# A transformer block on one core: key tiles by contraction halves, more transposes by DMA, and a new order

## The chip, the core and the metric

The kernel runs on one of the eight cores of a Trainium2 chip. The metric is device time in microseconds (us), the median of three runs, as reported for the core. TensorE (PE) multiplies, VectorE (DVE) and ScalarE (ACT) do elementwise work and move results out of PSUM, GpSimd (POOL) makes masks, and SyncE (SP) issues all DMAs. Each engine runs its own list of instructions strictly in order and waits for the others by semaphores.

## The reference, cut to what matters

The input x has 2048 tokens of width 512; the two weight chains are a linear attention with 32 heads of 16 and a dense layer of width 1792 with relu. All tensors are bf16.

```python
qkv = layernorm(x) @ wqkv
phi = lambda t: where(t > 0, t + 1, exp(t)) + 1e-6
pq, pk = phi(q), phi(k)
kv = einsum("bhsd,bhse->bhde", pk, v);  z = einsum("bhsd->bhd", pk)
o  = einsum("bhqd,bhde->bhqe", pq, kv) / (einsum("bhqd,bhd->bhq", pq, z) + 1e-6)
h  = x + merge_heads(o) @ wo
out = h + relu(layernorm(h) @ w1) @ w2
```

## The kernel before, in words

Tokens lie in 16 tiles of 128 and in four chunks (c) of 512. Every step is a small function `op_<name>`; the string ORDER (line 18) lists them as words, name and arguments joined by dots, and the loop in lines 548 to 550 calls them one after the other. A word goes to the engine that its operation uses, and each engine executes its own words in the order in which they stand. A scheduler doesn't come into it (line 92 sets a manual schedule). So ORDER is the whole plan: for each engine a queue, and between the queues the data dependences. PSUM has eight banks; the bank is an argument of the word, and a matmul that writes a bank waits until the last reader of its former contents is through.

The words of this text, with engine and line of the operation:

- lx.t.n loads n tiles of x (SP, L201); lk, lq, lv, lo, l1, l2 load weights (SP, L204).
- S.t, A.t: statistics of the first norm (DVE, L226, L227). R.t.n: its 1/sqrt, two ACT operations (L232, L233). N.t: the normalised tile ln_nat (DVE, L251).
- T.t.b transposes a normalised tile on PE, four 128x128 transposes into bank b (L270), and E.t (ACT, L280) or V.t (DVE, L283) copies it out into lnT. X.t does the same without PE: one transposing DMA (SP, L291).
- K.t.b: keys of a tile, four matmuls of 512 columns, one for each 128 of the contraction (L299). K.t.b.k.n does n of the four, beginning with k, so that a tile's keys can be cut into halves; the halves add up in the same bank.
- F, U, M, D: phi of the keys, exp and relu on ACT (L317, L320), min and add on DVE (L324, L327). qF, qU, qM, qD are the same for the queries; qW (DVE, L332) takes relu and add in one operation from PSUM and needs no qU.
- G.t: 512x512 sum over the tokens of normalised x times pk, four matmuls, in banks 4 to 7 (L351). The values are not computed for each token: kv (L392) multiplies G by the value weights afterwards, after gA (ACT) or gD (DVE, L387) moved G out. za, zf, z, zc, zh make the sums of the keys.
- Q.c.j.b: a quarter of the queries of a chunk, transposed, four matmuls (L307).
- dn.c.b: denominators of a chunk, 16 matmuls of 8 columns (L448); dnl, dnx (ACT, L454, L461) make the reciprocals, spread over the head's 16 columns, in rn (which lies in wk_sb); dt.t transposes a tile of them by DMA into rd (SP, L480). rt.t.b does that on PE (L270), and re.t (ACT, L472) copies it out. dm.c.jb.n (DVE, L484) multiplies two quarters of the queries by rd.
- m, mA, mD: kv times the output weights (L404). h.t.b: attention output of a tile, four matmuls (L494); hD (DVE, L500) adds x.
- s.t, a.t, r, n.t: second norm (DVE L228, L229, ACT L232, DVE L258). x.t transposes by DMA (SP, L292); t.t.b and e.t do it by PE and ACT (L286).
- p.c.f.b: first dense layer, four matmuls (L510); pA (ACT, L516) and pD (DVE, L521) apply the relu to two. f.t.b.f0.n: second dense layer (L530), in two halves of seven matmuls; fo (DVE, L538) scales and adds, fd (SP, L545) stores.
- warm.n.b: n matmuls of zeros ahead of the work (L215).

Of the kernel before, what the change touches and what calls it, by code (L numbers as in the profile page):

```python
# [15 lines left out]


ORDER = """
const table lx.0.1 lx.2.1 S.0 lx.1.1 S.2 A.0 S.1 A.2 R.0.1 N.0 R.2.1 lx.3.1 lk.0.2 lx.4.2 masks warm.1.7
warm.9.7 A.1 R.1.1 T.0.6 S.3 warm.1.7 N.2 T.2.4 N.1 A.3 E.0 R.3.1 T.1.5 lk.2.2 S.4 E.1 N.3 A.4 V.2 S.5 A.5  # L20
K.0.6 lx.6.2 K.1.3 T.3.1 F.0.1 U.0.1 lx.8.4 E.3 K.2.0 M.0.1 S.6 D.0.1 K.3.2 A.6 S.7 F.1.1 M.1.1 lx.12.4 R.4.2
N.5 A.7 N.4 U.1.1 D.1.1 F.2.1 U.2.1 R.6.2 S.8 S.9 N.7 A.9 A.8 M.2.1 N.6 lq.0.2 G.0 T.5.1 E.5 T.4.3 G.1 X.7
K.5.1 D.2.1 E.4 K.4.0 R.8.2 T.6.3 G.2 N.9 X.9 F.3.1 U.3.1 S.12 N.8 S.13 X.8 lq.2.2 M.3.1 A.13 A.12 D.3.1 E.6
K.6.2 F.4.2 R.12.2 U.4.2 K.7.3 G.3 M.4.2 S.11 F.6.2 U.6.2 N.12 D.4.2 S.10 S.14 N.13 M.6.2 A.11 A.10 D.6.2 A.14
R.10.2 X.12 K.9.1 G.4 N.11 S.15 N.10 A.15 X.13 K.8.0 G.5 G.6 za.2 U.8.2 F.8.2 X.11 X.10 G.7 R.14.2 K.13.1
K.12.0 M.8.2 N.15 D.8.2 za.4 N.14 K.11.3 K.10.2 G.8 l2.0.3 F.12.2 U.12.2 za.6 X.15 X.14 Q.0.0.0 F.10.2 Q.0.1.1
lv.2.2 l1.0.2 M.12.2 lv.0.2 l2.10.4 U.10.2 qU.0.0.2 qF.0.0.2 M.10.2 za.8 D.12.2 D.10.2 za.10 za.12 K.14.2 G.9
K.15.3 F.14.2 U.14.2 G.10 Q.0.3.1 Q.0.2.0 M.14.2 qF.0.2.2 qU.0.2.2 G.11 zf.12 D.14.2 G.12 z.0.2.14 z.2.2.14
z.1.2.14 z.3.2.14 qM.0.2.2 l2.7.3 lo.0.2 lo.2.2 l1.2.2 qM.0.0.2 qD.0.2.2 G.13 zc G.14 qD.0.0.2 zh dn.0.0 G.15
gD.2.2 gD.0.2 Q.1.1.3 Q.1.0.2 dnl.0 dnx.0.0.2 Q.1.2.0 dnx.0.2.2 kv.3.4 kv.0.4 kv.1.4 kv.2.4 Q.1.3.1 qF.1.0.2  # L30
qM.1.0.2 kx qF.1.2.2 qW.1.0.2 dt.0 dt.3 dt.2 dt.1 m.2.6 m.1.5 m.3.7 m.0.4 mA.0.2 Q.2.0.2 Q.2.1.3 qM.1.2.2
mA.2.2 qW.1.2.2 dn.1.5 dm.0.0.2 dm.0.2.2 dnl.1 dnx.1.2.2 Q.2.3.1 h.3.5 hD.3 h.0.6 h.1.7 hD.0 s.3 dnx.1.0.2
dt.6 Q.2.2.0 dt.4 dt.7 dt.5 qF.2.0.2 qU.2.0.2 h.2.6 hD.1 Q.3.0.2 Q.3.1.3 s.0 qF.2.2.2 qU.2.2.2 s.1 qU.3.0.2
a.3 a.0 hD.2 qM.2.0.2 n.0 a.1 n.1 dm.1.0.2 dm.1.2.2 n.3 s.2 Q.3.2.0 Q.3.3.1 qD.2.0.2 a.2 qM.2.2.2 n.2 qF.3.0.2
qF.3.2.2 l2.3.4 x.0 qM.3.2.2 qD.2.2.2 h.5.6 h.7.7 h.6.5 x.1 t.2.3 r.0.4 e.2 h.4.4 x.3 dn.2.3 dnl.2 dnx.2.0.2
p.0.0.2 dt.8 hD.6 qM.3.0.2 qW.3.2.2 hD.4 p.0.1.3 qD.3.0.2 hD.5 dnx.2.2.2 pA.0.0.2 p.0.3.1 p.0.2.0 dn.3.6
pD.0.2.2 p.0.5.3 p.0.4.2 pD.0.4.2 p.0.7.1 p.0.6.0 p.0.13.3 s.6 dt.10 p.0.12.2 dt.11 dt.9 hD.7 a.6 s.5 dm.2.0.2
dm.2.2.2 dnl.3 pA.0.6.2 a.5 pD.0.12.2 f.2.6.0.7 s.7 h.11.7 h.9.0 p.0.9.3 h.8.5 p.0.8.2 dnx.3.2.2 dnx.3.0.2
hD.9 a.7 hD.11 p.0.10.0 f.3.7.0.7 p.0.11.1 h.10.4 dt.15 pA.0.10.2 pD.0.8.2 dt.14 dt.13 dt.12 s.4 s.9 n.5
dm.3.2.2 s.11 hD.8 a.11 dm.3.0.2 hD.10 n.7 f.2.6.7.7 h.13.5 h.15.4 n.6 hD.15 a.4 n.4 s.8 h.14.1 f.3.7.7.7  # L40
h.12.2 f.0.4.0.7 x.5 x.6 s.10 hD.14 a.10 hD.13 hD.12 n.10 x.4 s.13 s.12 x.7 n.11 a.9 a.8 f.1.5.0.7 a.12 s.15
p.1.1.1 p.1.0.0 pA.1.0.2 f.1.5.7.7 a.15 s.14 fo.2 p.1.8.0 p.1.9.1 n.12 a.13 fo.3 n.15 n.13 fo.1 pD.1.8.2
f.0.4.7.7 a.14 n.8 p.1.12.0 p.1.13.1 p.1.2.2 p.1.3.3 p.1.10.6 r.12.4 r.4.4 pA.1.12.2 n.9 x.11 x.15 x.10 x.9
x.8 pD.1.2.2 p.1.7.5 p.1.5.1 fd.2 fd.3 p.1.4.0 p.2.3.3 p.2.2.2 n.14 fo.0 pD.1.4.2 pD.2.2.2 fd.0 x.13 x.14
p.2.0.0 p.1.11.7 p.2.7.3 p.2.1.1 r.8.4 pA.2.0.2 p.2.6.2 p.1.6.4 pD.2.6.2 p.2.4.0 pA.1.10.2 pA.1.6.2 p.2.5.1
pA.2.4.2 f.7.7.0.7 p.2.12.0 p.2.13.1 f.4.4.0.7 f.5.5.0.7 p.2.10.2 f.4.4.7.7 p.2.11.3 f.6.6.0.7 pD.2.10.2
pD.2.12.2 fd.1 x.12 f.6.6.7.7 f.5.5.7.7 p.2.8.0 p.2.9.1 p.3.2.2 p.3.3.3 fo.6 pD.2.8.2 fo.4 fo.5 p.3.4.0
f.7.7.7.7 p.3.5.1 pA.3.4.2 pD.3.2.2 fo.7 f.10.6.0.7 p.3.1.1 f.9.5.0.7 p.3.7.3 p.3.0.0 f.8.4.0.7 p.3.6.2 fd.6
f.9.5.7.7 f.11.7.0.7 f.10.6.7.7 fd.4 fd.5 fd.7 pA.3.0.2 pA.3.6.2 f.8.4.7.7 p.3.12.0 fo.9 f.11.7.7.7 p.3.13.1
p.3.11.3 p.3.10.2 pD.3.10.2 fo.8 fo.11 pA.3.12.2 p.3.9.1 f.13.5.0.7 p.3.8.0 f.12.4.0.7 pA.3.8.2 fo.10 fd.10  # L50
fd.9 f.13.5.7.7 f.14.6.0.7 fo.13 f.12.4.7.7 f.15.5.0.14.3.1 f.14.6.7.7 f.15.7.0.14.0.2 fd.13 fd.8 fd.11 fo.12
fo.14 fo.15.3.1 f.15.4.0.14.2.1 fd.12 fd.14 fd.15.3.1 fo.15.0.2 fo.15.2.1 fd.15.0.2 fd.15.2.1
"""


# [525 lines left out]
```

## Time and profile before

| What | Value |
|---|---|
| three runs | 170.04, 170.34, 170.82 us |
| median | 170.34 us |
| span of the profiled execution, first to last instruction | 168.6 us |
| what lies around the span, median less span | 1.74 us |
| DVE, ACT, POOL busy | 104.7, 64.3, 4.8 us |
| DMA moved | 15.36 MB |

All times in the trace are counted from the start of the span. A row of the chain of waits reads: start, length, what was running or being waited for. A row of the timeline reads: start, length, engine, line, operation, tiles, count, and in brackets the idle time of the engine before it and who ended it. A row of a group reads: line, engine, operation, tiles, shapes, count, then busy time, mean ns of one, then idle time before. A row of DMA issues ends with the median time from issue to landing. PE is TensorE's matmul row, PEld its weight loads, SPq the queue of SyncE.

### The profile page before, as it was taken

How to read it: one execution, taken by the hardware profiler on the slowest of the kernel's cores; microseconds unless marked ns; L12 is line 12 of the kernel's file. 1: busy time of each engine (PE TensorE's matmuls, PEld its weight loads, DVE VectorE, ACT ScalarE, POOL GpSimd, SP SyncE). 2: the span in 40 equal slices, each digit the busy share in tenths (PEclk: the TensorE clock that was granted, in tenths of full speed). 3: DMA queues.
4: the chain of work that ended last, by engine and by line, in shares of the span. 5: the costliest groups of instructions: out<-in, count | busy, mean ns of one | idle time of the engine just before them, and what ended most of it. 6: DMA issues, size and time to landing. Idle time of an engine off the chain costs nothing.

```text
span 168.6 us, 2307 instructions
## 1 busy us (share of the span) xinstructions
PE 163.1 (97%) x875; PEld 76.3 (45%) x875; DVE 104.7 (62%) x207; ACT 64.3 (38%) x97; POOL 4.8 (3%) x21
## 2 busy tenths in 40 slices
...
DMA packets 30091, 15.36 MB, mean 91 GB/s; under 512 B 22656, under 2 KB 29056, under 8 KB 30080
## 3 DMA queue, kind: packets, MB, share of 16 engines
...
q8 instruction: 7, 0.11, 0.3%
...
HBM read 7.86 MB, written 2.10 MB: 59 GB/s over the span
## 4 chain that ended last, share of the span: by engine, by line
PE 84%; ACT 4%; DMA 4%; SPq 3%; DVE 2%; issue 1%; DVEq 0%; ACTq 0%
PE bk L530 29%; PE bk L510 29%; PE bk L351 7%; PE bk L299 7%; PE bk L494 6%; PE bk L307 5%; DMA wk_sb<-in_A_wqkv_dram 3%; ACT eb L317 1%; DMA rd<-wk_sb 1%; SPq L201 1%; SPq L480 1%; PE bk L448 1%; ACT rb L320 1%; DVE pqT L332 1%; ACT lnT L280 1%
## 5 line engine op out<-in xcount | busy, mean ns | idle before, releaser
L530 PE MATMUL bk<-w_sb,at 128*128 128x512 bf16 (+2 forms) x252 | 51.5, 355 | 0.0
L510 PE MATMUL bk<-lnT,w_sb 128*128 128x512 bf16 x224 | 51.4, 379 | 0.0
L516 ACT ACTIVATE at<-bk 128x1024 bf16<-128x1024 f32 x14 | 14.1, 1023 | 70.3 <-PE bk L510 70.3
L521 DVE TENSOR_SCALAR at<-bk 128x1024 bf16<-128x1024 f32 x14 | 17.0, 1221 | 33.7 <-PE bk L510 33.7
L530 PEld LDWEIGHTS <-at 128*128 128x128 bf16 x252 | 23.6, 98 | 25.2
L510 PEld LDWEIGHTS <-w_sb 128*128 128x128 bf16 x224 | 21.8, 98 | 26.0 <-issue 0.2
L538 DVE SCALAR_TENSOR_TENSOR gT<-bk,rstd,h_nat 128x512 bf16<-128x512 f32 (+2 forms) x18 | 12.0, 686 | 18.3 <-PE bk L530 15.9
L317 ACT ACTIVATE eb<-bk 128x1024 bf16<-128x1024 f32 (+1 forms) x18 | 16.5, 925 | 6.1 <-PE bk L299 3.5
L299 PE MATMUL bk<-wk_sb,lnT 128*128 128x512 bf16 x64 | 15.5, 379 | 0.6 <-DMA wk_sb<-in_A_wqkv_dram 0.5
L494 PE MATMUL bk<-m_sb,pqs 128*128 128x512 bf16 x64 | 15.5, 379 | 0.1
L307 PE MATMUL bk<-lnT,wq_sb 128*128 128x512 bf16 x64 | 15.1, 379 | 0.1
L320 ACT ACTIVATE rb<-bk 128x1024 bf16<-128x1024 f32 (+1 forms) x15 | 13.6, 906 | 1.2 <-PE bk L307 1.2
L351 PE MATMUL bk<-at,h_nat 128*128 128x512 bf16 x56 | 13.7, 379 | 0.0
L500 DVE TENSOR_TENSOR h_nat<-bk,x_nat 128x512 bf16<-128x512 f32 x16 | 10.8, 678 | 2.7 <-PE bk L494 2.6
L226 DVE BATCH_NORM_STATS2 st<-x_nat 128x6 f32<-128x512 bf16 x16 | 10.6, 678 | 1.8 <-DMA x_nat<-in_A_x_dram 1.8
L228 DVE BATCH_NORM_STATS2 st<-h_nat 128x6 f32<-128x512 bf16 x16 | 10.5, 679 | 0.0
L299 PEld LDWEIGHTS <-lnT 128*128 128x128 bf16 x64 | 5.9, 98 | 8.2 <-ACT lnT L280 1.2
L494 PEld LDWEIGHTS <-pqs 128*128 128x128 bf16 x64 | 6.1, 98 | 7.9 <-DVE pqs L484 1.2
L307 PEld LDWEIGHTS <-wq_sb 128*128 128x128 bf16 x64 | 6.1, 97 | 7.3 <-issue 0.4
L351 PEld LDWEIGHTS <-h_nat 128*128 128x128 bf16 x64 | 6.0, 98 | 6.6
L461 ACT ACTIVATE wk_sb<-ld 128x1024 bf16<-128x1024 f32 x8 | 8.0, 1048 | 0.1
L324 DVE TENSOR_SCALAR eb<-eb 128x1024 bf16<-128x1024 bf16 (+1 forms) x18 | 6.9, 388 | 1.2 <-ACT eb L317 1.1
...
## 6 DMA issues: line engine op xcount, KB each, us to landing
...
wk_sb<-in_A_wqkv_dram SPq DMA_DIRECT2D x2, 256.0 KB, 3.7
x_nat<-in_A_x_dram SPq DMA_DIRECT2D x2, 256.0 KB, 4.1
```

The lines of the kernel that those rows point to most:

```text
L299: nc.tensor.matmul(bk[:, b, :], lhsT=lnT[c][:, kd, j * P : (j + 1) * P], rhs=wk_sb[:, kd, :], start=(kd == 0), stop=(kd == KD - 1),)
L307: nc.tensor.matmul(bk[:, b, :], lhsT=wq_sb[:, kd, j * P : (j + 1) * P], rhs=lnT[c][:, kd, :], start=(kd == 0), stop=(kd == KD - 1),)
L317: nc.scalar.activation(out=buf(eb, kind, i, n), in_=bank(at_bank[kind, i], n), func=ACT.Exp)
L320: nc.scalar.activation(out=buf(rb, kind, i, n), in_=bank(at_bank[kind, i], n), func=ACT.Relu)
L351: nc.tensor.matmul(bk[:, KD + kd, :], lhsT=ln_nat[:, t, kd * P : (kd + 1) * P], rhs=pk(t)[:, 0, :], start=(t == 0), stop=(t == NT - 1),)
L494: nc.tensor.matmul(bk[:, b, :], lhsT=pqs[:, (c * KD + jb) % NQ, j * P : (j + 1) * P], rhs=m_sb[:, jb, :], start=(jb == 0), stop=(jb == KD ...
L500: nc.vector.tensor_tensor(out=h_nat[:, t : t + n, :], in0=bank(at_bank["h", t], n), in1=x_nat[:, t : t + n, :], op=ALU.add,)
L510: nc.tensor.matmul(bk[:, b, cols], lhsT=w1_sb[:, kd, f * P : (f + 1) * P], rhs=lnT[c][:, kd, cols], start=(kd == 0), stop=(kd == KD - 1),)
L516: nc.scalar.activation(out=acts[c % 2][:, f : f + n, :], in_=bank(at_bank["p", c, f], n), func=ACT.Relu)
L521: nc.vector.tensor_scalar(out=acts[c % 2][:, f : f + n, :], in0=bank(at_bank["p", c, f], n), scalar1=0.0, scalar2=None, op0=ALU.max,)
L530: nc.tensor.matmul(bk[:, b, 0 : w * P], lhsT=acts[c % 2][:, f, j * P : (j + 1) * P], rhs=w2_sb[:, f, k * P : (k + w) * P], start=(f == 0), ...
L538: nc.vector.scalar_tensor_tensor(out=o_t[:, t % NO, cols], in0=bk[:, at_bank["f", t, k], 0 : w * P], scalar=rstd2[:, t : t + 1], in1=h_nat ...
```

## The change

Only ORDER is changed, in every line. Its parts:

- T.4, T.5, T.6 with their copies E.4, E.5, E.6 become X.4, X.5, X.6. Tile 2 is transposed first, and its copy is E.2 (ACT) in place of V.2 (DVE).
- K.0, K.1 and K.2 are cut into halves of two matmuls: first the first halves of tiles 2, 0, 1, then T.3, then the second halves, then K.3.
- t.2 with its copy e.2 becomes x.2. dt.1 and dt.2 become rt.1, re.1 and rt.2, re.2.
- One of two gD becomes gA, one of two mA becomes mD; qD.0.2 with qU becomes qW, and two qW become qU with qD; some pA and pD change places.
- The order of nearly all words is another, on PE, DVE, ACT and SP; the banks are assigned anew. lx.4.2 goes ahead of lk.0.2; lq.0.2 and lq.2.2 go behind X.12; the loads of wo, wv, w1 and w2 are put elsewhere between the transposes.

The words of the first part, before and after, cut to what the prediction speaks of:

```diff
-const table lx.0.1 lx.2.1 S.0 lx.1.1 S.2 A.0 S.1 A.2 R.0.1 N.0 R.2.1 lx.3.1 lk.0.2 lx.4.2 masks warm.1.7
-warm.9.7 A.1 R.1.1 T.0.6 S.3 warm.1.7 N.2 T.2.4 N.1 A.3 E.0 R.3.1 T.1.5 lk.2.2 S.4 E.1 N.3 A.4 V.2 S.5 A.5
-K.0.6 lx.6.2 K.1.3 T.3.1 F.0.1 U.0.1 lx.8.4 E.3 K.2.0 M.0.1 S.6 D.0.1 K.3.2 A.6 S.7 F.1.1 M.1.1 lx.12.4 R.4.2
-N.5 A.7 N.4 U.1.1 D.1.1 F.2.1 U.2.1 R.6.2 S.8 S.9 N.7 A.9 A.8 M.2.1 N.6 lq.0.2 G.0 T.5.1 E.5 T.4.3 G.1 X.7
-K.5.1 D.2.1 E.4 K.4.0 R.8.2 T.6.3 G.2 N.9 X.9 F.3.1 U.3.1 S.12 N.8 S.13 X.8 lq.2.2 M.3.1 A.13 A.12 D.3.1 E.6
...
+lx.2.1 table lx.0.1 const S.2 S.0 A.2 A.0 masks lx.1.1 R.2.1 lx.3.1 lx.4.2 S.1 lk.0.2 N.2 warm.9.5 A.1 R.0.1
+lk.2.2 lx.6.2 N.0 R.1.1 S.3 N.1 A.3 S.5 T.2.0 E.2 warm.1.5 T.0.3 S.4 A.5 T.1.2 E.0 K.2.0.0.2 lx.8.4 A.4 R.3.1
+E.1 N.3 lx.12.4 R.4.2 K.0.7.0.2 K.1.2.0.2 T.3.1 K.0.7.2.2 E.3 U.0.1 N.5 N.4 F.0.1 S.7 S.6 M.0.1 X.5 A.6 A.7 X.4
+K.2.0.2.2 K.1.2.2.2 U.1.1 D.0.1 R.6.2 S.9 N.6 S.8 K.3.3 warm.1.5 X.6 F.2.1 N.7 M.2.1 U.2.1 U.3.1 A.8 F.3.1 F.1.1
+D.2.1 A.9 G.0 M.3.1 S.12 X.7 R.8.2 K.5.1 N.9 K.4.0 D.3.1 G.2 X.9 K.6.2 F.4.2 G.3 K.7.3 N.8 S.13 A.12 M.1.1 U.4.2
+A.13 D.1.1 R.12.2 U.6.2 F.6.2 X.8 G.1 K.9.1 M.4.2 N.13 N.12 K.8.0 D.4.2 S.11 S.10 A.11 S.15 M.6.2 A.10 G.4 G.5
+X.13 X.12 F.8.2 R.10.2 U.8.2 D.6.2 M.8.2 lq.0.2 A.15 S.14 N.11 N.10 lq.2.2 G.7 A.14 X.11 X.10 za.2 lo.0.2 D.8.2
+K.13.2 R.14.2 K.12.1 G.6 G.8 K.11.3 za.4 U.12.2 F.12.2 N.14 N.15 M.12.2 za.6 lv.2.2 X.15 X.14 za.8 D.12.2 l1.2.2
...
```

The order of each engine is read from this by taking its words alone. SP's new order up to the first dt, and PE's from the queries of chunk 1 to the first p, are:

```
SP: lx.2 lx.0 lx.1 lx.3 lx.4 lk.0 lk.2 lx.6 lx.8 lx.12 X.5 X.4 X.6 X.7 X.9 X.8 X.13 X.12 lq.0 lq.2 X.11 X.10 lo.0 lv.2 X.15 X.14 l1.2 l1.0 lv.0 lo.2 dt.3 dt.0 l2.10 dt.4 dt.7 dt.6 dt.5 x.2 x.1 x.3 x.0
PE: z (4) G.14 G.15 dn.0 Q.1 (4) kv (4) rt.2 rt.1 Q.2.1 m (4) dn.1 Q.2.0 Q.2.3 h.2 h.1 h.3 Q.2.2 Q.3.3 h.0 Q.3.2 Q.3.1 Q.3.0 h.7 h.6 h.5 h.4 dn.2 p.0.1
```

PE's order before in the same stretch, from dn.0, was: dn.0 G.15 Q.1.1 Q.1.0 Q.1.2 kv (4) Q.1.3 m (4) Q.2.0 Q.2.1 dn.1 Q.2.3 h.3 h.0 h.1 Q.2.2 h.2 Q.3 (4) h.5 h.7 h.6 t.2 h.4 dn.2 p.0.0.

More of the change, by code (lines that the diff above doesn't have):

```diff
@@ L24 @@
[L24 to L52, printed above, removed]
+lx.2.1 table lx.0.1 const S.2 S.0 A.2 A.0 masks lx.1.1 R.2.1 lx.3.1 lx.4.2 S.1 lk.0.2 N.2 warm.9.5 A.1 R.0.1
@@ new lines @@
+X.13 X.12 F.8.2 R.10.2 U.8.2 D.6.2 M.8.2 lq.0.2 A.15 S.14 N.11 N.10 lq.2.2 G.7 A.14 X.11 X.10 za.2 lo.0.2 D.8.2
+K.13.2 R.14.2 K.12.1 G.6 G.8 K.11.3 za.4 U.12.2 F.12.2 N.14 N.15 M.12.2 za.6 lv.2.2 X.15 X.14 za.8 D.12.2 l1.2.2
+K.10.2 l1.0.2 lv.0.2 U.10.2 F.10.2 lo.2.2 Q.0.0.0 Q.0.1.1 G.9 K.15.3 M.10.2 K.14.2 qF.0.0.2 qU.0.0.2 D.10.2
+F.14.2 Q.0.2.0 Q.0.3.1 U.14.2 qF.0.2.2 G.13 G.11 G.12 za.10 za.12 M.14.2 G.10 qM.0.0.2 zf.12 D.14.2 z.0.3.14
+z.3.3.14 z.1.3.14 z.2.3.14 G.14 G.15 qD.0.0.2 qM.0.2.2 zc gA.0.2 qW.0.2.2 zh dn.0.2 Q.1.0.0 Q.1.1.1 dnl.0 gD.2.2
```

23 lines of the change are left out of this document (added).

## The prediction, made before the changed kernel was run

> **What bounds the kernel now.** I read the page's parts 1 and 4 first, then the whole chain of waits, then the busy time by stage.
>
> ```profile
> span 168.6 us, 2307 instructions
> ...
> PE 163.1 (97%) x875; PEld 76.3 (45%) x875; DVE 104.7 (62%) x207; ACT 64.3 (38%) x97; POOL 4.8 (3%) x21
> ```
> ```profile
> 13.75 1.90 PE bk L299 x8
> ...
> 44.38 0.69 DVE kvbd L400
> 45.07 1.14 DVE pqT L332
> 46.26 1.89 PE bk L307 x8
> ...
> 57.34 2.94 PE bk L494 x12
> 60.28 0.22 PE bk L270 x4
> ...
> 61.36 0.38 PE bk L448 x16
> 61.74 3.47 PE bk L510 x16
> ...
> 96.70 15.58 PE bk L510 x72
> ...
> 165.91 0.35 DVE gT L538
> ```
> ```profile
> 13.75:44.36 30.61, 30.61 (x185) 14.77 (x186) 27.87 (x58) 22.25 (x32) 0.00 (x0) 1.00 0.69 192
> 44.36:61.74 17.38, 17.22 (x109) 7.81 (x108) 15.45 (x31) 12.99 (x16) 0.00 (x0) 1.00 0.48 102
> 61.74:165.88 104.14, 104.13 (x525) 48.84 (x522) 50.36 (x85) 19.92 (x26) 0.00 (x0) 1.00 0.19 45
> ```
> The chain (start, length, what; all us) is TensorE without a break from 13.75, where K.5 begins, to 44.38, and again from 61.74, where the first p of the second matrix begins, to the end of the PE work at 165.9. In the stage table (length, then busy time by engine, PE first) the last stage is 104.13 busy of 104.14. So three things can move the time: when K.5 starts, what lies between it and the first p, and any new hole after that. A 512-wide matmul costs 15.58/72 = 0.216, a block of four 0.866, a tile transposed on PE 0.22, dn 0.38.
>
> Between 46.26 and 60.28 lie 14.02 us. The order has eight Q, seven h and one dn there, 15 blocks and 0.38: 15 x 0.866 + 0.38 = 13.37, so 0.65 us of holes, in front of and inside h.5. One more hole stands at 46.26: by
>
> ```profile
> 45.13 1.04 PE L404 MATMUL bk<-wo_sb,kvbd 128*128 128x512 bf16 x4
> ```
> the four m were through at 45.13 + 0.866 = 46.0, and Q.2.0 waited for qW.1.0 until 46.26: 0.27. Together 0.92 us of holes before the first p. Times come from one execution with a span of 168.6; the median of the runs is 170.34, so 1.74 lies around the span, and I add that to all forecasts.
>
> **The change, part by part.**
>
> *PE work.* T.4, T.5, T.6 and t.2 go (4 x 0.22), rt.1 and rt.2 come (2 x 0.22): -0.44. The K halves are the same matmuls in other places. All else on PE is the same count.
>
> *The start, up to K.5.* Durations and places from
>
> ```profile
> 4.12 1.42 SPq L201 DMA_DIRECT2D x_nat<-in_A_x_dram  x3
> ...
> 4.98 0.41 DVE L251 TENSOR_SCALAR h_nat<-x_nat,mv,rstd 128x512 bf16<-128x512 bf16 x1
> ...
> 5.45 0.40 PE L270 MATMUL bk<-ident,h_nat 128*128 128x128 bf16 x4 [0.35 <-DVE h_nat L251]
> ...
> 8.11 1.46 PE L299 MATMUL bk<-wk_sb,lnT 128*128 128x512 bf16 x6 [0.52 <-DMA wk_sb<-in_A_wqkv_dram]
> ...
> 11.35 1.03 PE L351 MATMUL bk<-pk_lo,h_nat 128*128 128x512 bf16 x4
> ```
> ```profile
> L226 DVE BATCH_NORM_STATS2 st<-x_nat 128x6 f32<-128x512 bf16 x16 | 10.6, 678 | 1.8 <-DMA x_nat<-in_A_x_dram 1.8
> L251 DVE TENSOR_SCALAR h_nat<-x_nat,mv,rstd 128x512 bf16<-128x512 bf16 x16 | 6.3, 401 | 0.0
> L280 ACT ACTIVATE lnT<-bk 128x512 bf16<-128x512 bf16 x6 | 3.4, 587 | 0.2 <-PE bk L270 0.2
> L320 ACT ACTIVATE rb<-bk 128x512 bf16<-128x512 f32 x4 | 2.4, 589 | 0.0
> ```
> Tile 2 takes the place of tile 0: N.2 4.98, T.2 5.45. N.0 comes one rstd later (5.44), N.1 behind S.3 (6.35), T.1 6.8. K's first halves run from 7.05, E.1 holds the third to 8.0; T.3 waits for N.3, which stands behind S.5 and S.4 (8.13 to 8.54). From 8.85 the six second halves and K.3 follow (10 x 0.216): 11.0. The halves thus end the wait for the second half of wk (8.11, quoted), but only 0.35 earlier than now (G.0 starts at 11.35), since T.3 is late next. One warm-up and G.0, which waits for D.0 (E.3, U.0, F.0 in a row on ACT at 0.59 each, then M.0, D.0), end at 12.3. PE is then 0.58 ahead: now it has G.1 (0.87) more done at 13.75, and 12.3 + 0.87 = 13.17.
>
> *The wait that is added.* K.5 and K.4 no longer take a PE transpose and an ACT copy, but X.5 and X.4, which SP issues behind all x loads. N.5 ends at 9.2 (R.4 holds it), so X.5 is issued at 9.25. What it finds ahead of it:
>
> ```profile
> DMA to landing us min/median/max: 2.2/3.0/8.2
> ```
> ```profile
> wq_sb<-in_A_wqkv_dram SPq DMA_DIRECT2D x1, 256.0 KB, 4.3
> ```
> ```profile
> lnT<-h_nat SPq DMA_TRANSPOSE x1, 4.0
> ```
> ```profile
> 17.99 0.57 SPq L204 DMA_DIRECT2D wq_sb<-in_A_wqkv_dram  x1
> 18.84 3.37 SPq L291 DMA_TRANSPOSE lnT<-h_nat  x2
> ```
> ```profile
> lnT<-h_nat SPq DMA_TRANSPOSE x9, 2.5
> ```
> The first row is that of the x loads: the slowest, lx.12.4, third of the three issued from 4.12 (so at 5.07), landed after 8.2, at 13.3. The next rows are the one case now in which a transpose follows a load: lq.2.2, issued 17.99, landed at 22.29; X.12, issued 18.84, took 4.0 instead of the median 2.5 and landed at 22.84, 0.55 behind the load. So I take X.5 to land 0.55 behind lx.12.4, 13.85, less 0.2 because lq.0.2 (256 KB) no longer draws on memory beside it: 13.65. Bounds: 11.75 (2.5 after its issue, no queueing) and 15.8 (a full 2.5 behind the load). PE stands from 12.3 to 13.7 with G.2, K.6, G.3 and all else queued behind K.5. X.4 follows within the 0.87 that K.5 takes.
>
> *K.5 to the first p.* Now this takes 61.74 - 13.75 = 47.99. Less the 0.92 of holes, plus G.1 (0.87), plus rt (0.44), less T.6 and t.2 (0.44): 47.94, so equality is at a K.5 start of 13.80. I followed every PE wait in the new order with the durations of the groups. The narrow ones, as margin between producer and PE: D.8 before G.8 0.6; zh before dn.0 0.1 (z end, zc, qW.0.2 1.22 and zh 0.28 against G.14 and G.15 1.73); qD.1.2 before dn.1 0; dm.0 before h.2 0.2; dt.5 and dm.1 before h.7 0.4 (the hole of now, filled by Q.3.0, which moved behind h.0); hD.0 before Q.3.0 0.7. One fails: x.0 before p.0.1. dt.4 can be issued 0.47 after h.2 starts; its three followers at 1.21 each and 2.5 for the last bring dm.1 to +6.1, two dm, s.0, a.0 and n.0 take 2.6, x.0 another 2.5: +11.2, against PE's 13 blocks and dn, 11.13 after the same point: 0.1 to 0.15 of stall. Sources:
>
> ```profile
> L332 DVE SCALAR_TENSOR_TENSOR pqT<-bk,eb 128x1024 bf16<-128x1024 f32 x3 | 3.7, 1219 | 0.1
> L484 DVE TENSOR_TENSOR pqs<-pqT,rd 128x1024 bf16<-128x1024 bf16 x8 | 5.2, 682 | 0.7 <-DMA rd<-wk_sb 0.7
> L228 DVE BATCH_NORM_STATS2 st<-h_nat 128x6 f32<-128x512 bf16 x16 | 10.5, 679 | 0.0
> ```
> ```profile
> L480 SPq DMA_TRANSPOSE rd<-wk_sb x16: 1189/1212/1265, 41.5 to 75.7; - x16
> ```
> The Trainium skill, page "Advanced Engine Details and Errata", section "X-Bar Transpose (TRN2)", says that transposing DMAs are as fast as regular ones. SP's 1.21 a transpose against 0.47 a plain load (1.42/3) here speaks against it, at the issue at least; at 0.47 the last of the four dt would be issued 3 x 0.74 = 2.2 earlier, the 0.15 would vanish, and the sum would be 0.15 lower.
>
> *First p to the end.* The same p, f, h and dn.3 in another order. Buffers of PSUM come free with at least 0.4 to spare in my walk (tightest: pD.2.6 before p.3.5, pD.3.0 before f.12). DVE is busy 50 of 104 there, so nothing piles up. I cost it at 0; if one margin is gone, some 0.5 each. The tail has the same three pieces (256, 128, 128 wide) and the same last store: 0.
>
> *Sum.* K.5 at 13.70 against 13.80, plus 0.15: +0.05 on the span, 168.65, and with 1.74 around it 170.4: no change (0.5%, 0.85 us, is about what can be told from none).
>
> **The rivals.**
>
> *A, the forecast:* the hole before K.5 eats what the halves, the removed transposes and the filled holes give: 170.4, chance 0.47; 169.6 to 171.1.
>
> *B, X.5 hardly waits.* If the loads' tail is shorter without lq.0.2, K.5 starts with G.0's end at 12.35; then G.2 waits 0.35 for D.2 (S.9 waits for lx.8.4, then N.6, S.8, N.7, M.2). 12.35 + 0.35 + 0.15 - 13.80 = -0.95: 169.4. Against it stands the 0.55 row; for it that the tail is of a few engines only. Chance 0.20.
>
> *C, slower: a second queueing.* lo.0.2 and lv.2.2 are now issued right ahead of X.15 and X.14, whose K come at once.
>
> ```profile
> wq_sb<-in_A_wqkv_dram SPq DMA_DIRECT2D x2, 256.0 KB, 6.3
> wv_sb<-in_A_wqkv_dram SPq DMA_DIRECT2D x2, 256.0 KB, 4.0
> ```
> lv.2.2 is issued at 27.2 (X.11 and X.10 hold SP from 24.2 to 26.6), lands after 4.0 to 6.3, at 31.2 to 33.5, and X.15 0.55 later, 31.75 to 34.05, while K.15 is due 13.70 + 18.2 = 31.9: 0 to 2.15 of stall, 1.2 in the middle: 171.6. It decides from a landing later than 4.2 after issue. Before, X.15 had l2.0.3 ahead and was used 6 us after. Chance 0.28.
>
> *D, the clock.* If X.5 lands at the upper bound, PE stands 3.4 us. The first warm-ups ran slower than 0.216:
>
> ```profile
> 1.25 3.85 PE L215 MATMUL bk<-m_sb 128*128 128x512 bf16 x10 [1.25 <-DVE ones L177]
> ```
> 0.385 each. If PE fell back to that for as long (3.85 us), it would lose 1.7 on top of 15.8 - 13.8 = 2.0: 174.1. The granted clock of the stages quoted is 1.00, and no gap now is near this length. Chance 0.05. The Trainium skill, "TensorE: Matmul & The Clock Gate", Part 1, gives this as a rule: an idle window of about 3.4 us halves the clock; no run here shows it.
>
> **How the numbers follow.** Faster by over 0.5% is B: 0.20. Within: A, 0.47. Slower: C and D, 0.33. The range leaves out D, the worst of C and the best of B: 169.3 to 171.7.
>
> **What would show it.** In the profile after: the wait of K.5's weight load (L299) for the transpose, near 12.3 to 13.7; G.0 at about 11.4; no wait before h.7 and Q.2.0; a short one of L510 for lnT near 61.8; PE without a hole afterwards. I am wrong if X.5 lands before 12.5 or after 14.5, if K.15 or K.14 wait, or if p and f stop for a buffer.

## The result, and the profile after

The changed kernel took **171.50 us** (median of eight runs, 171.07 to 172.21), the kernel before beside it 170.03 (eight runs, 169.82 to 170.82): ratio 1.0070, 95% interval 1.0047 to 1.0094. It is slower by a little more than the half per cent that was called no change; the time lies inside the range given, near its upper end. Measured once more later, unchanged, it was 1.0031 (1.0008 to 1.0054). So it costs 0.3 to 0.7%; what is known of the difference between the two figures comes below (e5).

The page of the changed kernel, its first part and the row of its instruction queue (packets, MB, share of 16 DMA engines):

```profile
span 170.1 us, 2279 instructions
...
PE 162.1 (95%) x851; PEld 76.1 (45%) x867; DVE 107.9 (63%) x208; ACT 62.7 (37%) x95; POOL 4.7 (3%) x21
...
q8 instruction: 7, 0.11, 0.3%
```

The profiled execution has a span of 170.1 against 168.6. PE has less work, as meant, and is idle longer. Where, the stage table tells (start and end, length, then busy time by engine, PE first; cut where K.5 begins, where the first p begins and where the PE work ends):

```profile
0.00:13.75 13.75, 10.59 (x48) 4.02 (x48) 10.10 (x32) 8.86 (x23) 4.72 (x21) 1.00 0.80 210
13.75:62.22 48.47, 47.82 (x291) 23.22 (x298) 44.09 (x90) 35.72 (x48) 0.00 (x0) 1.00 0.53 136
62.22:166.46 104.24, 103.70 (x514) 48.86 (x524) 53.33 (x88) 18.09 (x26) 0.00 (x0) 1.00 0.23 57
166.46:170.10 3.64, 0.00 (x0) 0.00 (x0) 0.35 (x1) 0.00 (x0) 0.00 (x0) 0.89 0.22 60
```

Before, the same four lengths were 13.75, 47.85, 104.27 and 2.69; the end, and the row with the first p:

```profile
61.60 0.59 PE L510 MATMUL bk<-lnT,w_sb 128*128 128x512 bf16 x2
```
```profile
165.88:168.60 2.72, 0.00 (x0) 0.00 (x0) 0.35 (x1) 0.00 (x0) 0.00 (x0) 0.93 0.15 38
```

(The prediction cut at 61.74, where the record of dn ends; the first p had begun at 61.60, as the records of two matmuls overlap. Here both kernels are cut at its start.) So 0.62 us came in between K.5 and the first p, nothing in the long last stage, and 0.94 behind the last matmul, where nothing had been forecast. (Some matmul records are missing in the trace after, so "busy" is a little low there.) The chain of waits shows the front part, first as a whole, then the stretch before the first p:

```profile
9.76 3.94 DMA lnT<-h_nat
...
19.96 1.81 PE bk L299 x8
...
62.22 5.55 PE bk L510 x25
...
161.90 4.56 PE bk L530 x48
```
```profile
61.52 0.38 PE bk L448 x16
61.91 0.31 issue
62.22 0.81 PE bk L510 x3
```

K.5 waits for X.5 until 13.75, as forecast; K.9 and K.8 take 1.81 for eight matmuls that cost 1.73; and PE stands 0.31 in front of the first p, for x.0 (landed 62.12). The wait costs more than the 0.31 of the chain: from the first matmul of dn to the first p it was 0.40 before and is 0.85 now, so 0.45. The tail, from the timeline (in brackets the idle time of the engine and what ended it), and the row of one store by itself:

```profile
161.15 6.80 SPq L545 DMA_DIRECT2D out_dram<-gT  x8
163.54 0.75 DVE L538 SCALAR_TENSOR_TENSOR gT<-bk,rstd,h_nat 128x512 bf16<-128x512 f32 x1 [2.42 <-DMA out_dram<-gT]
...
166.48 0.35 DVE L538 SCALAR_TENSOR_TENSOR gT<-bk,rstd,h_nat 128x128 bf16<-128x128 f32 x1 [0.43 <-PE bk L530]
```
```profile
165.81 1.17 SPq L545 DMA_DIRECT2D out_dram<-gT  x1
```

and before, the last store:

```profile
166.29 0.33 SPq L545 DMA_DIRECT2D out_dram<-gT  x1
```

The last fo is done at 166.83 (before: 166.26, and the last store went out 0.03 later). The last store should go out then; it goes out at 167.56, since SP needed 1.17 us to issue fd.13 at 165.81 (0.33 to 0.45 is usual for these stores), and fd.15.3.1 and fd.15.2.1 stood behind it. What ran at that time besides, by the DMA table of the window 165.6 to 166.7:

```profile
q1 hardware_dynamic: 138, 0.06, 21.1%
q8 instruction: 1, 0.02, 5.0%
```

One packet of 16 KB of instructions: 5.0% of 16 engines for 1.1 us is 0.88 us on one DMA engine. In the trace it runs from 165.72 to 166.60, and fd.13's issue ends at 166.98.

### The profile page after: what moved, and what is told of

Same layout as the page of the kernel before. It is cut to its first block, busy times and chain, and to the rows that moved or that the text cites. A ratio compares the mean times of both kernels' runs of the same rounds, so it can differ in the third digit from the quotient of the medians.

```text
span 170.1 us, 2279 instructions
## 1 busy us (share of the span) xinstructions
PE 162.1 (95%) x851; PEld 76.1 (45%) x867; DVE 107.9 (63%) x208; ACT 62.7 (37%) x95; POOL 4.7 (3%) x21
## 4 chain that ended last, share of the span: by engine, by line
PE 89%; DMA 4%; DVE 3%; issue 1%; ACT 0%; SPq 0%
PE bk L530 29%; PE bk L510 28%; PE bk L307 8%; PE bk L494 8%; PE bk L351 8%; PE bk L299 6%; DMA lnT<-h_nat 2%; DVE st L226 2%; DMA x_nat<-in_A_x_dram 2%; PE bk L448 1%; DVE h_nat L251 1%; PE bk L392 1%; PE bk L404 1%; DVE mv L227 0%; PE bk L270 0%
## 5 line engine op out<-in xcount | busy, mean ns | idle before, releaser
L510 PE MATMUL bk<-lnT,w_sb 128*128 128x512 bf16 x219 | 50.4, 379 | 0.5 <-issue 0.3
L530 PE MATMUL bk<-w_sb,at 128*128 128x512 bf16 (+2 forms) x248 | 50.3, 355 | 0.3
L516 ACT ACTIVATE at<-bk 128x1024 bf16<-128x1024 f32 x12 | 12.2, 1022 | 54.8 <-PE bk L510 54.8
L521 DVE TENSOR_SCALAR at<-bk 128x1024 bf16<-128x1024 f32 x16 | 19.5, 1222 | 18.7 <-PE bk L510 18.5
L320 ACT ACTIVATE rb<-bk 128x1024 bf16<-128x1024 f32 (+1 forms) x16 | 14.4, 917 | 4.0 <-PE bk L299 3.5
L351 PE MATMUL bk<-at,h_nat 128*128 128x512 bf16 x55 | 13.2, 379 | 0.1
L228 DVE BATCH_NORM_STATS2 st<-h_nat 128x6 f32<-128x512 bf16 x16 | 11.0, 685 | 0.1
```

The source lines that it names most:

```text
L320: nc.scalar.activation(out=buf(rb, kind, i, n), in_=bank(at_bank[kind, i], n), func=ACT.Relu)
L351: nc.tensor.matmul(bk[:, KD + kd, :], lhsT=ln_nat[:, t, kd * P : (kd + 1) * P], rhs=pk(t)[:, 0, :], start=(t == 0), stop=(t == NT - 1),)
L510: nc.tensor.matmul(bk[:, b, cols], lhsT=w1_sb[:, kd, f * P : (f + 1) * P], rhs=lnT[c][:, kd, cols], start=(kd == 0), stop=(kd == KD - 1),)
L516: nc.scalar.activation(out=acts[c % 2][:, f : f + n, :], in_=bank(at_bank["p", c, f], n), func=ACT.Relu)
L521: nc.vector.tensor_scalar(out=acts[c % 2][:, f : f + n, :], in0=bank(at_bank["p", c, f], n), scalar1=0.0, scalar2=None, op0=ALU.max,)
L530: nc.tensor.matmul(bk[:, b, 0 : w * P], lhsT=acts[c % 2][:, f, j * P : (j + 1) * P], rhs=w2_sb[:, f, k * P : (k + w) * P], start=(f == 0), ...
```

## The experiments

Two theories of the tail were tested against each other. **Theory I**: PE's instructions come by DMA, in packets of 16 KB, about one for every 250 PE instructions; a packet holds up the DMAs that meet it, and SP with them. **Theory O**: the new order of stores is at fault, with a full store between the last pieces. Beside these, single steps of the prediction were tried. All times in one table; "K.5", "first p" (starts of their first matmuls) and "tail" (end of PE to end of span) are of each kernel's profiled execution:

| Kernel | median us | before beside it | ratio (95%) | K.5 | first p | tail |
|---|---|---|---|---|---|---|
| before | 170.03 | | | 13.75 | 61.60 | 2.69 |
| changed | 171.50 | 170.03 | 1.0070 (1.0047 to 1.0094) | 13.75 | 62.22 | 3.63 |
| e1 store order | 170.43 | 169.94 | 1.0021 (1.0002 to 1.0039) | 13.13 | 61.64 | 2.89 |
| e2 transfers moved | 173.26 | 169.94 | 1.0180 (1.0155 to 1.0204) | 13.49 | 63.95 | 2.88 |
| e3 lx.12.4 late | 172.13 | 169.94 | 1.0117 (1.0090 to 1.0144) | 12.44 | 62.79 | 3.12 |
| e4 p cut | 170.21 | 169.94 | 1.0013 (0.9997 to 1.0029) | 12.95 | 60.95 | 2.98 |
| e5 changed again | 170.95 | 170.31 | 1.0031 (1.0008 to 1.0054) | 13.16 | 61.53 | 3.13 |
| e6 six matmuls more | 170.56 | 170.31 | 1.0012 (0.9993 to 1.0031) | 13.61 | 61.77 | 2.89 |
| e7 e1 and e4 | 170.35 | 170.31 | 0.9997 (0.9979 to 1.0015) | 12.81 | 61.12 | 3.01 |
| e8 before, transfers moved | 171.40 | 170.31 | 1.0037 (1.0007 to 1.0067) | 14.14 | 62.17 | 2.70 |
| e9 one store by ACT | 170.55 | 169.98 | 1.0033 (1.0014 to 1.0053) | 12.47 | 61.45 | 2.86 |
| e10 e7, stores by ACT | 170.23 | 169.98 | 1.0019 (0.9998 to 1.0039) | 12.91 | 60.89 | 2.87 |
| e11 whole K | 172.72 | 169.98 | 1.0142 (1.0100 to 1.0185) | 14.66 | 63.37 | 3.22 |
| e12 before, one store by ACT | 170.07 | 169.98 | 1.0000 (0.9980 to 1.0020) | 13.91 | 61.79 | 2.71 |

### e1: the stores in another order

```diff
-fd.10 ... fo.9 ... fo.8 fd.8 fo.11 fo.12 fo.14 ... fd.14 fd.9 fd.11 fd.12 fo.13 fo.15.0.2 ...
-fo.15.3.1 fo.15.2.1 fd.15.0.2 fd.13 fd.15.3.1 fd.15.2.1
+fd.10 ... fo.9 fd.9 ... fo.8 fd.8 fo.11 fd.11 fo.12 fd.12 fo.14 ... fd.14 fo.13 fd.13 fo.15.0.2 ...
+fo.15.3.1 fo.15.2.1 fd.15.0.2 fd.15.3.1 fd.15.2.1
```

> The changed kernel with another order of SP's last stores alone: fd.9, fd.11, fd.12 and fd.14 each right behind its own fo, fd.13 ahead of the three pieces of tile 15. In the changed kernel 3.6 us lay between the end of the PE work (166.46) and the end of the span, 2.68 before the change; fd.13, issued at 165.81 between the pieces, held SP for 1.17 us instead of 0.33 to 0.45, and the last store went out at 167.56, 0.72 after its fo was done (166.84). Theory O (order: a full store between the last pieces holds SP): the last store goes out at 166.9, span 0.7 shorter, about 170.8. Theory I (instruction transfer: the page lists one 16 KB transfer of queue q8, instructions, and it ran from 165.72 to 166.60, when the long issue stood): whatever store meets it is held up, here fd.15.3.1, ready at 166.06, to about 166.95; the last store goes out at 167.0 to 167.3: 0.3 to 0.5 gained, 171.0 to 171.2. If neither, 171.5.

Measured: 170.43. The tail is 2.89 and the last store goes out with its fo (166.29 for 166.26), as theory O has it; but SP is held here too, by the store that meets the packet (164.92 to 165.80), now fd.15.3.1:

```profile
165.51 0.67 SPq L545 DMA_DIRECT2D out_dram<-gT  x1
```

It ended at 166.18, just before the last store was ready. So the held issue follows the packet, not fd.13; with this order it is over before the last store is ready. The time fell by 1.07, more than the tail can give: K.5 began 0.62 earlier than in the changed kernel's profile, with the same words up to there. That called for e5.

### e2: the instruction packets moved by 28 pairs

```diff
-warm.9.5
+warm.1.5 warms.36.5
```

(warms.n.b is n matmuls of zeros with 64 columns.)

> The changed kernel with eight of its nine first warm-up matmuls (512 columns) replaced by 36 of 64 columns: 28 more pairs of weight load and matmul in PE's queue, about as long in time, the stores untouched. The q8 instruction transfers come about every 250 PE instructions in both traces, so the last one should come some 6 us earlier, near 160, where SP issues nothing. Theory I: fd.13's issue takes 0.33 to 0.45, the last store goes out at about 166.9, span 0.7 shorter, about 170.8. Theory O: the issue between the pieces is long as before, 171.5. The start has 0.36 us of PE idle before K.5 as a cushion, in case the warm-ups take longer.

Measured: 173.26, far from both. For the tail theory I holds: the last packet ran from 162.27, met the other stores only, fd.13 went out in 0.43, tail 2.88, last store 0.03 behind its fo, with the order of stores that theory O blames. But the other packets moved too, and one (60.10 to 61.52) met the transposes that the first p waits for. Rows of SP's queue, of the chain and of the DMA table of 59.9 to 61.6:

```profile
60.44 2.15 SPq L292 DMA_TRANSPOSE lnT<-hn  x1
```
```profile
60.44 3.42 DMA lnT<-hn
63.86 0.09 issue
63.95 1.24 PE bk L510 x5
```
```profile
q1 hardware_dynamic: 502, 0.12, 92.6%
q8 instruction: 1, 0.02, 5.2%
```

x.0 took 2.15 to issue instead of 1.21 and 3.42 to land instead of 2.44; x.3 ahead of it landed after 4.14. PE stood 1.3 us for it. Another packet (17.67) met X.9 and X.8 (3.73 and 3.80 instead of 2.42 and 3.32), and PE stood 0.7 us there. The same mechanism that ate the end of the changed kernel can eat its middle.

Not all of the loss is the packets'. The 36 short matmuls were over at 3.78, PE then stood until 5.45, and what followed went at half pace until 9.73, six matmuls of the keys at 0.43 each and not 0.216:

```profile
5.45 0.61 PE L270 MATMUL bk<-ident,h_nat 128*128 128x128 bf16 x4 [1.68 <-DVE h_nat L251]
...
7.17 2.77 PE L299 MATMUL bk<-wk_sb,lnT 128*128 128x512 bf16 x6
```

(The column of the granted clock reads 1.00 there; the pace is read from the matmuls.) So K.5 began with the end of G.0 at 13.49, though X.5 had landed at 12.09: 0.3 later than in e5 below, of the 2.4 us by which this span (171.3) is longer than that of e5.

### e3: lx.12.4 behind X.4

```diff
-E.1 N.3 lx.12.4 R.4.2 ... X.5 A.6 A.7 X.4 K.2.0.2.2 ... M.3.1 S.12 X.7 ... N.8 S.13
+E.1 N.3 R.4.2 ... X.5 A.6 A.7 X.4 lx.12.4 K.2.0.2.2 ... M.3.1 X.7 ... N.8 S.12 S.13
```

> The changed kernel with the load lx.12.4 issued behind X.5 and X.4 instead of ahead of them (S.12 moved behind N.8 on DVE, so that DVE doesn't stand for it). Theory of the forecast: X.5 landed at 13.70 because it was queued behind lx.12.4 (last part landed 12.93). Now it lands 2.5 after its issue or 0.8 behind lx.8.4 (11.62), about 12.4; K.5 starts with G.0's end at 13.23, 0.5 earlier, and PE stays ahead: 171.0. Rival 1: X.5's 3.9 us is its own or comes from the loads before; K.5 at 13.7, 171.5. Rival 2: K.5 is earlier, but G.2 or K.6 behind it then wait (X.6 now queues behind lx.12.4), and the first p comes at 62.2 as now: 171.5 or more.

Measured: 172.13. X.5 landed 2.51 after its issue, at 11.76, and K.5 began with G.0's end at 12.44: the forecast's account of X.5 (behind the last x load) holds. But rival 2 has the result: the load now stands ahead of X.6, which lands after 4.39. Timeline of PE, then the chain:

```profile
12.44 1.89 PE L299 MATMUL bk<-wk_sb,lnT 128*128 128x512 bf16 x8
...
17.02 1.04 PE L299 MATMUL bk<-wk_sb,lnT 128*128 128x512 bf16 x4 [1.82 <-DMA lnT<-h_nat]
```
```profile
12.58 4.39 DMA lnT<-h_nat
```

A queueing behind 512 KB was only handed from X.5 to X.6, where it costs more.

### e4: p.0.1 cut in two

```diff
-dn.2.5 dnl.2 p.0.1.6 hD.4
+dn.2.5 dnl.2 p.0.1.6.1.2 p.0.1.6.0.2 hD.4
```

> The changed kernel with the first block of p, p.0.1, cut into two halves of 256 columns, tiles 2 and 3 first: only the second half (0.43 us later) needs x.0. Theory: the 0.31 us that PE stood before the first p was x.0's landing alone; the first p starts at about 61.9, and the end of the PE work comes 0.3 earlier, 166.15: 171.2, if the tail stays. Rival: the wait only moves into the block, or something later waits instead: end of PE at 166.46. Four more pairs of PE instructions also bring the last instruction transfer some 0.9 us forward, to 164.9 to 165.7: by theory I the store issued then (fd.15.0.2 or fd.13) is the long one; by theory O it is fd.13 again.

Measured: 170.21. The wait for x.0 is gone: x.0 landed at 61.29, 0.34 after PE had begun with the other half. But the stage behind it is 0.24 longer than in the other kernels (104.23):

```profile
60.95:165.42 104.47, 104.47 (x534) 49.35 (x530) 53.74 (x88) 18.36 (x26) 0.00 (x0) 1.00 0.23 57
```

since part of the rival came true as well: PE loses 0.09 before the block of p at 62.77, right behind an hD that ends at 62.72, and 0.13 inside dn.3, at 69.0; the changed kernel has neither. So the cut nets about 0.1 to 0.2 and not the 0.3 expected; the rest of the gain over 171.50 came from the start (K.5 at 12.95) and the tail, where the packet (164.07 to 164.95) held fd.13 for 0.53 only.

### e5: the changed kernel once more

> The changed kernel once more, not altered. The two store and block edits gained 1.07 and 1.29 us, more than the 0.72 and 0.31 that they were meant to take out, and in their profiles K.5 began at 13.13 and 12.95 where the changed kernel's profile has 13.75, with the same words up to there: the first loads landed sooner (second half of wk 9.66 in the changed kernel's profile). Theory S: that profile had a slow start by chance, and the kernel's median belongs to it only in part; now K.5 at about 13.0 and a median near 171.0. Theory N: the slow start belongs to this kernel; K.5 at 13.7 again, 171.5.

Measured: 170.95, ratio 1.0031. Theory S: K.5 at 13.16.

```profile
0.00:13.16 13.16, 10.55 (x47) 4.21 (x48) 10.09 (x32) 9.00 (x23) 4.72 (x21) 1.00 0.78 219
13.16:61.53 48.37, 47.76 (x290) 23.28 (x297) 43.92 (x89) 35.47 (x48) 0.00 (x0) 1.00 0.53 137
61.53:165.76 104.23, 103.70 (x514) 48.90 (x524) 53.35 (x88) 18.12 (x26) 0.00 (x0) 1.00 0.24 57
165.76:168.90 3.14, 0.00 (x1) 0.00 (x0) 0.35 (x1) 0.00 (x0) 0.00 (x0) 1.00 0.25 70
```
```profile
165.13 0.69 SPq L545 DMA_DIRECT2D out_dram<-gT  x1
```

In this execution, the shortest of its twelve (spans 168.9 to 169.6), PE ends at 165.76, 0.1 before the kernel before, and the whole loss against 168.6 is the tail: fd.13 held again, from 165.13 to 165.82, 0.37 after the packet's end (164.57 to 165.45). The first profile was later from the first loads on: the second half of wk landed at 9.66 there, at 7.55 here. Why the loads land 2 us apart in executions of one program was not settled, and neither was how many of the first eight runs had the late loads.

### e6: six small matmuls in front of K.5

```diff
-G.0 M.3.1
+G.0 warms.6.1 M.3.1
```

> The changed kernel with six matmuls of 64 columns of zeros between G.0 and K.5, where PE waits for X.5 anyway (0.36 us): 12 more PE instructions, nothing else. Theory I (the 16 KB instruction transfers of PE, one about every 250 of its instructions, hold up the DMAs that meet them): the last transfer comes 1.3 us earlier, at 164.4 to 165.3, ahead of fd.15.0.2 at 165.4; no store is held up, fd.13 issues in 0.42 and the last store goes out with its fo: the tail (end of PE to end of span) is 2.7 to 2.9 instead of 3.63, 0.7 gained. Theory O (order of the stores): the tail stays at 3.6. The transfer at 43.44 comes at 42.1 to 43.3: dt.3, issued at 43.2, takes 1.2 to 1.5 instead of 1.86.

Measured: 170.56, 0.39 less than e5 beside it, by adding work. The packet ran from 164.25 to 165.39, so it came 0.3 and not 1.3 us earlier, and was longer than expected (1.14). It met fd.15.0.2 alone; fd.13 began 0.03 before its end and took its usual time:

```profile
165.36 0.43 SPq L545 DMA_DIRECT2D out_dram<-gT  x1
```
```profile
166.00:168.90 2.90, 0.00 (x0) 0.00 (x0) 0.35 (x1) 0.00 (x0) 0.00 (x0) 1.00 0.27 75
```

Tail 2.89, last store 0.03 behind its fo: theory I, since order and stores are those of e5, where it was 3.13. The packet near 43 came earlier too (41.83 to 43.23), and dt.3 took 1.19 to issue and not 1.86, as expected. The gain of the medians (0.39) is clear run for run (170.25 to 170.79 here, 170.60 to 171.44 in e5, twelve each beside each other), but the profiles don't explain it: both spans are 168.9, since the 0.24 gained in this tail was lost by a PE that ended 0.23 later.

### e7: e1 and e4 together

> The order of stores of the first experiment and the cut p.0.1 of the fourth together. If both edits took out what they were meant to, and do not share it: PE ends at 165.4 as in the fourth, the last store goes out with its fo, tail 2.7: span 168.1, 169.8 us, level with the kernel before (169.94). If the gain of the two was one and the same (a luckier place of the instruction transfers), 170.2.

Measured: 170.35, ratio 0.9997: level with the kernel before, as expected if both edits did what they were meant to. PE ended at 165.59; the packet (164.05, here 1.58 long) held fd.15.3.1 for 0.78, and the tail is 3.01, not 2.7.

### e8: the kernel before with its packets moved

```diff
-warm.9.7
+warm.7.7 warms.17.7
```

> The kernel before, with two of its nine main warm-up matmuls replaced by 17 of 64 columns (2 x 0.43 against 17 x 0.059 us, so the same time): 15 more pairs in PE's queue, nothing else. Theory I: the instruction transfers come 3.2 us earlier, at about 17.2, 37.4, 59.3, and 159.3. The third then meets the transposes x that the first p waits for (issued 55.98 to 58.53, landed by 61.25): they land 1 to 2 us later and the first p, 61.6 to 61.7 now, starts at 62.3 to 63.2; the last meets three full stores at 159.1 to 159.9, and a fo waits. 170.6 to 171.5. Rival: the number of PE instructions ahead has no effect on the time: 169.9.

Inconclusive. The third packet came at 61.56, not 59.3 (so the count of PE instructions ahead does not set its time alone), so it missed the transposes x. The first, at 16.75, met two X, which took 3.85 and 4.22 instead of 2.44 and 2.45; PE lost 0.2 there. The rest of its 0.5 us is a K.5 at 14.14 (13.75 in the kernel before, 13.91 in e12); whether the warm-ups or the loads made that, this run does not tell. Nor is the profile typical: four of the twelve runs took 169.97 to 170.85, the profiled one among them, and eight took 171.06 to 171.85. What the eight met isn't known; a third packet among the transposes isn't ruled out.

### e9: fd.13 issued by ACT

```diff
+    def op_fa(t, k=0, w=KD):
+        cols = slice(k * P, (k + w) * P)
+        nc.scalar.dma_start(out=of_v[:, t, cols], in_=o_t[:, t % NO, cols])
...
-fd.15.0.2 fd.13 fd.15.3.1
+fd.15.0.2 fa.13 fd.15.3.1
```

> The changed kernel with one store, fd.13, issued by ACT (idle by then) instead of SP. In five runs so far the first store that SP issued while an instruction transfer ran went out in 0.33, and the next was held until 0.37 us after the transfer's end (166.60 to 166.98 in the changed kernel's first profile; 165.45 to 165.82 in its second, where the tail is 3.13 against 2.69 before). Theory I in the form 'SP is held by what already stands in its own queue': ACT issues fd.13 in 0.33 to 0.45 at about 164.1, fd.15.3.1 follows fd.15.0.2 at its own time; if the transfer still runs then, it is the second store of SP in it and is held, ends at 165.9, and the last store goes out with its fo: tail 2.7 to 2.8, 0.3 to 0.4 less than the changed kernel; the median 0.1 to 0.2 above the kernel before instead of 0.5. Rival: a second issuing engine doesn't help, since the held one is the DMA engine: tail 3.1.

Measured: 170.55, ratio 1.0033: no gain in time over the changed kernel (1.0031) can be seen, with intervals that are wider than the gain expected, though the profile shows what theory I expected of the tail, 2.86, no store held. The profile also shows why an early start helps so little. X.5 landed sooner here and K.5 began at 12.47; of the 0.7 gained on e5 only 0.1 is left at the first p: it is gone at K.8, which waits for X.8. Weight loads of PE, and the DMA table of 18.4 to 20.0:

```profile
19.98 0.55 PEld L299 LDWEIGHTS <-lnT 128*128 128x128 bf16 x4 [0.93 <-DMA lnT<-h_nat]
```
```profile
q1 hardware_dynamic: 642, 0.15, 48.1%
q14 instruction: 1, 0.01, 1.2%
```

In all kernels with this start X.8 took 3.3 us to land and not 2.42, with 15 of its 16 parts there after 2.5, and in all of them a packet of the other instruction queue (0.3 to 0.6 us) ran while it was under way; in e3 and in the kernel before, where it ran later, X.8 took 2.44 and 2.45. That the packet is the cause is an inference from this coincidence. The first p came 41.47 to 41.48 after K.8 in e1, e9 and the changed kernel alike.

### e10: e7 with three stores by ACT

```diff
-fd.14 ... fd.13 ... fd.15.0.2 fd.15.3.1 fd.15.2.1
+fa.14 ... fa.13 ... fd.15.0.2 fa.15.3.1 fd.15.2.1
```

> Order of stores of the first experiment, cut p.0.1, and three of the last stores (fd.14, fd.13, fd.15.3.1) issued by ACT, the other two pieces by SP. So no engine issues two in a row inside one instruction transfer. PE end at 165.4 to 165.6 as in the other kernels with the cut; tail 2.7: span 168.1 to 168.3, 0.2 to 0.4 below the version without ACT (which was level with the kernel before): 0.1 to 0.2% faster than the kernel before. Rival: as in the run beside, no gain by ACT: level.

Measured: 170.23, ratio 1.0019, beside e7's 0.9997: the intervals overlap, no gain is seen. No store was held (all 0.33 to 0.37), yet:

```profile
165.37:168.24 2.87, 0.00 (x0) 0.00 (x0) 0.35 (x1) 0.00 (x0) 0.00 (x0) 0.94 0.15 33
```

2.87 and not 2.7 is thus the tail of the new order without any held store. Of the missing 0.17 the trace shows the place: from the last landing to the end of the span it takes 0.99 to 1.01 in the changed kernel and all its variants, 0.83 in the kernel before, e8 and e12. SP waits there for the semaphores of the stores, two at a time in a fixed order, 0.063 apart; the last store's is in the last pair in the kernel before, and in the changed one three more pairs follow it. This was read from the rows, not tried.

### e11: the first three keys whole

```diff
-... E.0 K.2.0.0.2 ... K.0.7.0.2 K.1.2.0.2 T.3.1 K.0.7.2.2 E.3 ... K.2.0.2.2 K.1.2.2.2 ... K.3.3
+... E.0 ... T.3.1 K.0.7 E.3 ... K.2.0 K.1.2 ... K.3.3
```

> The changed kernel with the keys of tiles 2, 0 and 1 whole again (K.0, K.2, K.1 where the second halves stood). The prediction had the halves earn 0.35 us at G.0, and the wait of K.5 for X.5 (0.5 in the second profile) swallow it. Theory: PE now stands from the transposes (7.2) to E.3's tile and begins K.0 with wk's second half (7.6); the twelve matmuls end about 0.5 to 1.3 later than now, G.0 at 12.1 to 12.9 instead of 11.6, and K.5 at 13.2 to 13.9 instead of 13.16: 0 to 0.7 slower than the changed kernel. If K.5 stays at 13.16 the halves earn nothing here. Three pairs of PE instructions stay the same in number, so the instruction transfers stay.

Measured: 172.72, 1.1% more than the changed kernel's 1.0031. G.0 began at 13.79 instead of 11.63, K.5 at 14.66. Not the order alone did that. Timeline of PE, then the stage table, cut where the granted TensorE clock (the column behind the engines) changes:

```profile
8.61 0.61 PE L270 MATMUL bk<-ident,h_nat 128*128 128x128 bf16 x4 [1.38 <-DVE h_nat L251]
9.02 4.72 PE L299 MATMUL bk<-wk_sb,lnT 128*128 128x512 bf16 x16
```
```profile
4.43:7.84 3.41, 1.72 (x15) 0.77 (x13) 3.41 (x11) 3.08 (x11) 1.66 (x5) 1.00 0.98 288
7.84:11.25 3.41, 2.64 (x10) 1.27 (x11) 2.65 (x8) 1.53 (x5) 0.00 (x0) 0.50 0.87 295
11.25:13.79 2.54, 2.54 (x13) 1.13 (x12) 1.36 (x5) 1.65 (x5) 0.00 (x0) 1.00 0.62 87
```

PE stood 1.38 us for N.3 with nothing to do (until 8.61). At 7.84, in the middle of that, the clock was halved, for 3.41 us: sixteen matmuls took 4.72, where 16 x 0.216 and the 0.16 by which the last record is longer make 3.62. With the halves in that place (e5) the clock stayed at 1.00. How often it fell the six runs tell: four have a mean clock of 0.99 and took 172.6 to 173.3 us, two have 1.00 and took 171.5 and 171.6. So the clock is worth about 1.4 us where it falls, and the other order without it about 0.6 (against the 170.95 of e5, measured at another time).

### e12: the kernel before with one store by ACT

```diff
-fd.15.0.2 fd.15.2.1
+fa.15.0.2 fd.15.2.1
```

> The kernel before with one of its last pieces, fd.15.0.2, issued by ACT: a control for the two runs with ACT. In the profile before, the last instruction transfer (162.51 to 163.39) met no issue of a store and the tail is 2.69. Theory I: nothing to gain, tail 2.6 to 2.8, level with the kernel before. Rival: a second issuing engine shortens any tail by the 0.38 of an issue: 0.2% faster.

Measured: ratio 1.0000 (0.9980 to 1.0020), tail 2.71. Theory I: where no packet meets the last stores, there is nothing to gain.

## Why the prediction was partly right

**The range was right, the likeliest case was not.** Forecast: a span of 168.65 and no change. Measured: 170.1 (first profile) and 168.9 (second), slower by 0.7 and 0.3%. Of the 1.4 us between 168.65 and the first profile 0.94 lie behind the last matmul, 0.5 between K.5 and the first p, and almost nothing at K.5. The step that failed most is the one costed at nothing: "The tail has the same three pieces (256, 128, 128 wide) and the same last store: 0." The pieces are the same; what stands between them and when the packet of instructions comes is not. The tail cost 0.94 in the first profile and 0.44 in the second, of which 0.7 and 0.2 are the last store held behind fd.13 and 0.17 the end of the span. The prediction called the slower side rival C (K.15 behind lv.2.2). That one did not happen: lv.2.2 landed 3.05 after its issue, X.15 and X.14 after 3.02 and 2.55, and neither K.15 nor K.14 waited. That the time lies in the range is therefore partly luck: the range was stretched for rival C, and what made the time longer was not in it.

**X.5.** Mechanism right, size near its place: it lands 0.62 to 0.77 behind lx.12.4 (0.55 taken), at 13.70 in the first profile (13.65 forecast) and between 12.4 and 13.3 in seven others with the same words up to there, as the loads land. That the first profile hit the forecast is luck of its late loads. e3 shows that without the load ahead it lands at 11.76. The row that the 0.55 came from was a mixed one: X.12 of the kernel before also had a packet of instructions in its flight (20.43 to 21.36). In e8, where this packet came earlier, X.12 took 2.91 and not 4.0, and landed 0.59 behind its load, so the 0.55 holds. Rival B's early K.5 came in six of the seven profiles with this start, in e9 without any wait for X.5, but not its 169.4, because of the next point.

**K.5 to the first p.** The work was nearly right: 47.94 forecast; e4 and e10, where PE hardly stops, took 48.14 and 48.13 by the same measure, to the end of dn's record. What was missed is K.8, which can't start before X.8 lands at 19.8 to 20.2 (20.69 in the first profile); a K.5 ahead of about 13.0 is wasted there. The wait for x.0 was foreseen, but mis-sized: 0.1 to 0.15 forecast, 0.45 measured. From the issue of dt.4 (50.52) x.0 landed after 11.6 and not 11.2; the three dt behind it took 3.86 to issue and not 3.63, and from dt.5's landing to x.0's issue it was 2.83 and not 2.6. Of the hole at h.7, said to be filled, 0.08 is left, inside the block. The holes at Q.2.0 and in h.5 are gone.

**First p to the end.** 104.27 became 104.23, both from the start of the first p: costed right.

**The halves.** They were priced at 0.35 at G.0, with T.3 as the next wait. That weighed their order only. In the place that the new order gives them they also keep PE busy through the wait for N.3, and with it the clock: in e11's profile G.0 is 2.16 later without them, 1.1 of it by sixteen matmuls at the lower clock. (That kernel is not the placement of before, which had T.2 and K.0 elsewhere, so this prices the halves within the new order.) The Trainium skill, page "TensorE: Matmul & The Clock Gate", Part 1, has the clock fall to half after about one idle window of 3.4 us. The trace agrees with half (0.50) as the value, and the stretch at half is 3.41 us long; but PE was busy for 1.72 of the 3.41 us before the fall, so here a window partly filled was enough.

**The packet.** In seven profiles a full or partial store was caught (changed, e1, e3, e4, e5, e7, e11): the store issued by SP as the packet began or while it ran took 0.33, the next was held, until 0.37 to 0.39 after the packet's end. In e2, e6, e10 and e12 no second one by SP stood well inside it, and none was held; in e9 a second one began 0.07 before its end, took 0.33, and so was not held. The Trainium skill, page "DMA: Bandwidth & Descriptors", section "Queues, rings and completion order", says that a DMA engine takes turns between the queues and finishes a whole packet before it goes to the next. The trace agrees: of fd.15.0.2, issued at 165.43 in the changed kernel, 15 of 16 parts had landed by 166.97, and the last at 167.78. That the issuing engine is held as well the page does not say; the runs show it. That the packets' place decides is shown by e6 and e2 in the profiles; in the times e6 is 0.39 better than e5, for which the profiles give no account, and e9, without the held store, measured no better than the changed kernel.

**Open:** why the first eight runs lie 0.55 above the second twelve. The first profile puts 0.6 on late loads at the start and 0.5 on a longer tail. The spans of all eight are 169.4 to 170.5, those of the twelve 168.9 to 169.6, so the two profiles differ more (170.1 and 168.9) than the medians do; what the other seven met isn't known.
